# Two segments' scores in one pair of PSUM banks, block means in steps, and a newly computed order

## Chip, core and metric

The kernel runs on one core of one Trainium2 chip. The metric is device time in microseconds (us); three runs of the kernel before gave 614.13, 614.66 and 614.96, median 614.66.

## What is computed

The reference is attention followed by two feed-forward stages, in fp32. q, k and v have 2 batches, 8 heads, 768 positions and 64 elements a head.

```python
block, window = (32, 16)
k_sum = k.reshape(B, H, nb, block, D).max(axis=3)
v_sum = v.reshape(B, H, nb, block, D).mean(axis=3)
scores_l = scale * np.matmul(q, k.transpose(0, 1, 3, 2))
mask_l = np.abs(pos[:, None] - pos[None, :]) < window
scores_s = scale * np.einsum('bhsd,bhnd->bhsn', q, k_sum) + np.log(block)
...
a = softmax over the masked scores_l and the scores_s together
attn = np.matmul(a, np.concatenate([v, v_sum], axis=2))
x = attn.transpose(0, 2, 1, 3).reshape(1536, 512)
...
x = (silu(x @ w_gate) * (x @ w_val)) @ w_out        # 1536 wide inside
h = x @ w_in                                        # 2048 wide inside
out = np.where(h >= 1, h, np.where(h <= -1, 0, (h + 1) ** 2 / 4)) @ w2_out
```

Each position attends to the 31 positions within its window and to 24 block summaries: the maximum of each block of 32 keys, and the mean of each block of 32 values. So a query tile of 64 positions has 96 columns of local scores and 24 columns of block scores (KN = 120).

## The kernel before

**Tiling.** The 1536 rows are three chunks of 512. A chunk consists of two segments of 256 positions (a segment may belong to either batch), and a segment of four query tiles of 64. Heads go in four pairs p = 0 to 3. Chunk 0 goes through attention first; its two feed-forward stages run while TensorE's gaps take the attention of chunks 1 and 2. Afterwards chunks 1 and 2 go through the feed-forward stages together.

**Attention jobs** of batch b, segment s and pair p (`segment_jobs`): sc, the scores (L604: 16 matmuls into two banks, one bank for each head of the pair); mx, mask and maxima (DVE, L617); ex, the exponentials (ACT, L629); iv, sums and reciprocals; no, the normalisation (L642, DVE or POOL); wt, the transposes of the weights (L650, tile pt); pt, their copy out of the bank (tile pT); av, the product with the values (L559, tile px); xh and xl, its copy (tile x) and the remainder (tile xl). Ahead of the first segment of a batch and pair stand kl, ko, kp, kt, km and kc (`head_jobs`): load of the keys, reordering (tile kord), transposes (L496, tile pk), their copies, the block maxima and their broadcast.

**Block means of the values** (`vmean`, tile pv, L468): matmuls with a matrix of averages add up, in one bank, the means of all four pairs, each pair in its own 32 partitions. vo (`vmean_out`) copies a pair's 24 rows out of the bank (four copies a batch, with a ring of three tiles), and ve (`vmean_put`) writes them beside the values of each window (24x1024).

**Weights.** They come as 64-bit numbers. A pack of two 128-wide units is loaded (raw), turned into fp32 by high (ACT, L833), low (ACT or DVE) and bits (DVE, L842, tile wb), kept in DRAM for the later chunks, and split into a rounded part hi and a remainder lo (L865, POOL or DVE, tile wA). Every product is three matmuls: hi with hi, hi with lo, lo with hi (`mm3`, L926). The first pack holds the gate and value units 0 of the first stage, and its products (tiles pg and pv) are 256 columns wide and run for each half of the chunk.

**Order.** Nothing is left to run-time choice: every engine executes its own queue in order. The queues are written by a planner (`Plan.emit`), which takes, again and again, the ready job with the lowest start plus `urge` times rank; ranks are sums of numbers from the table T (L24 on). Jobs that write PSUM take a bank from a ring and give it back when named readers are done: for chunks 1 and 2 all attention jobs share banks b2 and b3, and the products of the weights' columns use b0 and b1 (row products accumulate in y0 to y3). Where the planner expects TensorE to stand idle ahead of a job that takes a bank, it puts transposes of an identity matrix there (`bank`, L296), as fillers.

```python
if engine == "PE" and chosen and len(takes[0]) > 1:
    self.pad = min(self.PAD_MOST, int(max(0.0, idle - self.SLACK) / self.PAD_US))
```

## Time and profile before

| | |
|---|---|
| median of three runs | 614.66 us |
| the profiled execution: time | 613.92 us |
| its span, first to last instruction | 612.2 us |
| busy: TensorE matmul (PE) | 602.9 us, 98% |
| busy: VectorE (DVE) / ScalarE (ACT) / GpSimd (POOL) | 481.8 / 371.3 / 61.8 us |
| TensorE's granted clock, mean | 0.994 |
| chain that ended last | PE 95%, ACT 2%, DVE 1%, POOL 1% |

The page gives one execution of the program. "Busy" counts an instruction from start to end; matmuls overlap, so the cost of one matmul in a row is the distance between starts. An fp32 matmul stands in the trace as two records, so "sc x16" there is 8 matmuls of the program. The chain of the end is followed back from the last instruction: each step to what released it, or to the instruction before it on its engine. The time that is not in the span, 1.7 us here, belongs to the launch.

### The profile page before, as it was taken

Reading aid. Unit: us, or ns where it says so; the run is one execution under the profiler, and the core shown is the slowest. Engines: PE = TensorE matmul, PEld = TensorE weight load, DVE = VectorE, ACT = ScalarE, POOL = GpSimd, SP = SyncE. Lnnn points to the kernel's source line nnn. Section 1 sums busy time; section 2 is a strip of 40 time slices with the busy share of each in tenths; the row PEclk is TensorE's granted clock in tenths of the full one; section 3 lists DMA queues with packets and bytes.
Section 4 is the critical chain, followed back from the end, with each engine's and each line's share of the span. In section 5 each row is a group of like instructions: output and inputs, shape, how many; then the busy total and the mean of one; then the engine's idle time right before and its main releaser. Section 6 shows DMA issues by size and latency. Waiting matters only on the chain.

```text
span 612.2 us, 9565 instructions
## 1 busy us (share of the span) xinstructions
PE 602.9 (98%) x3583; PEld 496.1 (81%) x3583; DVE 481.8 (79%) x869; ACT 371.3 (61%) x670; POOL 61.8 (10%) x73
## 2 busy tenths in 40 slices
PE   7999999999999999999999999999999999999997
PEld 6888877787778888888888888888888888888886
DVE  6689789788889999898897788867798975846662
ACT  6798887787987794665544453532268575646212
POOL 5131012012000000010010000100010220100000
PEclk9799999999999999999999999999999999999999
DMA  9999998779874997123210213233211111013311
GB/s 226 293 324 237 345 323 285 269 268 293 307 278 147 312 349 255 69 77 130 70 69 1 69 70 103 104 103 104 70 34 70 37 67 34 35 34 112 130 35 69
DMA packets 77150, 94.99 MB, mean 155 GB/s; under 512 B 34224, under 2 KB 60080, under 8 KB 77104
## 3 DMA queue, kind: packets, MB, share of 16 engines
q1 hardware_dynamic: 77104, 94.39, 48.7%
q8 instruction: 28, 0.46, 0.3%
q14 instruction: 18, 0.15, 0.1%
HBM read 73.40 MB, written 20.97 MB: 154 GB/s over the span
## 4 chain that ended last, share of the span: by engine, by line
PE 95%; ACT 2%; DVE 1%; POOL 1%; issue 0%; ACTq 0%; POOLq 0%; DVEq 0%
PE acc_y L926 38%; PE qi L926 12%; PE qg L926 9%; PE qv L926 9%; PE pi L926 7%; PE pv L926 6%; PE pg L926 6%; PE pt L650 2%; PE px L559 2%; PE sc L604 1%; PE pk L496 1%; ACT big L629 1%; PE pq L540 1%; ACT big L385 1%; PE pk L296 1%; POOL wA L865 0%
## 5 line engine op out<-in xcount | busy, mean ns | idle before, releaser
L926 PE MATMUL acc_y<-dd,h 128*128 128x512 f32 (+1 forms) x387 | 88.7, 387 | 0.0
L926 PEld LDWEIGHTS acc_y<-dd,h 128*128 128x128 f32 x387 | 72.4, 188 | 14.9
L926 PE MATMUL acc_y<-h,dd 128*128 128x512 f32 x288 | 66.4, 389 | 0.0
L926 PEld LDWEIGHTS acc_y<-h,dd 128*128 128x128 f32 x288 | 54.1, 188 | 11.2
L385 ACT ACTIVATE dd<-wf 128x1024 fp32r<-128x1024 f32 x28 | 29.5, 1056 | 54.8 <-PE acc_y L926 54.8
L926 PE MATMUL acc_y<-wA,h 128*128 128x512 f32 x192 | 45.9, 390 | 0.0
L926 PE MATMUL qi<-xj,wjs 128*128 128x512 f32 x192 | 45.4, 390 | 0.0
L926 PE MATMUL pi<-y,wA 128*128 128x512 f32 x128 | 42.6, 393 | 0.0
L842 DVE SCALAR_TENSOR_TENSOR wb<-dd 128x1024 int32<-128x1024 int32 x34 | 41.4, 1220 | 1.4 <-ACT dd L833 0.7
L865 DVE TENSOR_TENSOR wA<-wb,wA 128x1024 fp32r<-128x1024 f32 x32 | 39.5, 1234 | 3.6 <-ACT wA L385 2.9
L926 PEld LDWEIGHTS qi<-xj,wjs 128*128 128x128 f32 x192 | 36.0, 188 | 7.8 <-DVE xj L865 0.4
L926 PEld LDWEIGHTS acc_y<-wA,h 128*128 128x128 f32 x192 | 36.0, 188 | 7.5
L833 ACT ACTIVATE dd<-raw 128x1024 f32<-128x1024 f32 x34 | 38.7, 1140 | 1.1 <-DMA raw<-in_moe_w_out_dram 0.9
L926 PE MATMUL acc_y<-h,wA 128*128 128x512 f32 x144 | 37.0, 401 | 0.0
L926 PE MATMUL qg<-xj,wjs 128*128 128x512 f32 x144 | 36.3, 390 | 0.0
L926 PE MATMUL qv<-xj,wjs 128*128 128x512 f32 x144 | 36.2, 389 | 0.0
L926 PE MATMUL pg<-x,wA 128*128 128x512 f32 (+1 forms) x112 | 35.9, 375 | 0.3 <-POOL wA L865 0.3
L926 PE MATMUL pv<-x,wA 128*128 128x512 f32 (+1 forms) x112 | 35.7, 375 | 0.0
L926 PE MATMUL qi<-xj,wjo 128*128 128x512 f32 x144 | 35.1, 389 | 0.0
L865 POOL TENSOR_TENSOR dd<-wf,dd 128x1024 fp32r<-128x1024 f32 x5 | 12.8, 2553 | 198.9 <-ACT dd L385 133.5
L865 DVE TENSOR_TENSOR h<-r,h 128x512 fp32r<-128x512 f32 x42 | 30.1, 717 | 2.8 <-ACT h L385 1.8
L926 PEld LDWEIGHTS qg<-xj,wjs 128*128 128x128 f32 x144 | 27.0, 188 | 5.8 <-DVE xj L865 0.2
(165 smaller groups left out, 1263.2 us busy)
## 6 DMA issues: line engine op xcount, KB each, us to landing
raw<-in_moe_w_out_dram SPq DMA_DIRECT2D x14, 1024.0 KB, 7.3
raw<-in_moe_w_in_dram SPq DMA_DIRECT2D x16, 512.0 KB, 5.6
wf<-kept_z SPq DMA_DIRECT2D x16, 512.0 KB, 3.2
raw<-in_moe_w_gate_dram SPq DMA_DIRECT2D x12, 512.0 KB, 6.2
raw<-in_moe_w_val_dram SPq DMA_DIRECT2D x12, 512.0 KB, 7.1
kept_g<-wb SPq DMA_DIRECT2D x12, 512.0 KB, 5.8
wj<-kept_g SPq DMA_DIRECT2D x12, 512.0 KB, 4.7
wf<-kept_o SPq DMA_DIRECT2D x12, 512.0 KB, 3.3
```

The costliest lines, as they stand in the source:

```text
L296: nc.tensor.transpose(t[:, 0:P], ident, ident)
L385: nc.scalar.activation(out, in_, AF.Copy, scale=scale)
L496: nc.tensor.transpose(cols[:, r], kraw[b, p][one, r].rearrange("p h d -> p (h d)"), ident[one, one])
L540: nc.tensor.transpose(pq[:, r * P:(r + 1) * P], raw[:, r].rearrange("p h d -> p (h d)"), ident)
L559: nc.tensor.matmul(px[h * D:(h + 1) * D, col:col + QT], vwin[0:KN, w, 2 * p + h], pT[0:KN, 2 * h + w // 2, w % 2 * QT:(w % 2 + 1) * QT], s ...
L604: nc.tensor.matmul(scs[h][j * QT:(j + 1) * QT, w // 2], qT[head, (w + j) * QT:(w + j + 1) * QT], kwin[p][head, s * WPS + w + j], start=Tru ...
L629: nc.scalar.activation(sm[:, w], sm[:, w], AF.Exp, bias=mx[:, 0, w:w + 1], scale=-1.0, **more)
L650: nc.tensor.transpose(pt[0:KN, w * P:(w + 1) * P], v_["sm"][:, w], ident)
L833: nc.scalar.activation(x[:, 0], raws[k][:, :, :, 1].bitcast(F32), AF.Prelu, scale=2.0 ** -112, alpha=2.0 ** 32)
L842: nc.vector.scalar_tensor_tensor(b, x[:, 0], 3, x[:, 1], op0=ALU.logical_shift_left, op1=ALU.bitwise_or)
L865: e.tensor_tensor(out, a, b, op=ALU.subtract)
L926: nc.tensor.matmul(dst, lhs(a), rhs(b), start=first and i == 0, stop=last and i == 2, **more)
```

## The change

1. **Scores.** Segment (1, 2, p) puts its scores behind those of (1, 1, p) in the same two banks, and (0, 2, p) for p = 1 to 3 behind those of (1, 0, p-1) (`beside`). The second job takes no bank, is ranked directly behind the first, and the banks come free when the maxima of both are done. (0, 2, 0) and (1, 0, 3) have no partner, and the segments of chunk 0 are left as they were.
2. **Means.** For batch 0 the matmuls of the means are three jobs, one for each loaded segment of values and one for the rest, in one bank that is held meanwhile. The matrices of averages are 32 columns wide instead of 24, so that all 128 partitions of the bank are written, and vo is one copy of 128x128 for a batch; its ring of tiles is gone.
3. **Order.** All numbers of T are new but those of `rings`, `handoff`, `order`, `pack` and `wide`, so every queue is in a new order.

The core of the diff (line numbers of L468 and below move by 1 to 8, those of the weights' code by 30):

```diff
--- before.py
+++ after.py
@@ -23,76 +23,76 @@
 T = {'rings': {'sm': 4, 'raw': 3, 'dd': 2, 'wf': 3, 'wA': 4, 'h': 3},
...
- 'urge': 0.00048,
- 'weight': (0.57, 8.439, 0.171, 0.404),
+ 'urge': 0.00044,
+ 'weight': (0.581, 190.813, 0.102, 0.425),
...
@@ -284,7 +284,7 @@
     BANKS, ACCS = ("b0", "b1", "b2", "b3"), ("y0", "y1", "y2", "y3")
     plan = Plan({
         **{r: 1 for r in (*BANKS, *ACCS, *SLOTS)}, "kraw": 2, "kord": 1,
-        "qT": 2, "vm": 3, **T["rings"],
+        "qT": 2, **T["rings"],
     })
     job = plan.job
 
@@ -335,10 +335,10 @@
         return out
 
     carved = carve(
-        "big0", (NPAIR, (NTILE, KN)), (1, (3, KN)), (1, (2 * NB,)), (4, (WPS, 2)),
+        "big0", (NPAIR, (NTILE, KN)), (1, (3, KN)), (4, (WPS, 2)),
         (2, (WPS, KN + 1)))
-    kwin, masks, tavg = carved[:NPAIR], carved[NPAIR], carved[NPAIR + 1]
-    dens, smx = carved[NPAIR + 2:NPAIR + 6], carved[NPAIR + 6:]
+    kwin, masks = carved[:NPAIR], carved[NPAIR]
+    dens, smx = carved[NPAIR + 1:NPAIR + 5], carved[NPAIR + 5:]
     smx += [const.tile([P, WPS, KN + 1], F32, name=f"sm{i}") for i in range(2, T["rings"]["sm"])]
     nc.vector.memset(masks[:, :, KW:], LN_BLOCK / scale)
     nc.vector.memset(masks[:, :, 0:KW], 0.0)
@@ -353,8 +353,8 @@
                     base=WINDOW + sgn * off, pattern=[[-sgn, KW]], channel_multiplier=sgn,
                 )
     carved = carve(
-        "big1", (1, (2 * WPS, H, D)), (2, (CH,)), (2, (2, S // P, D)), (3, (2 * D,)), (1, (2, 2 * NB)))
-    vall, qTs, kraws, vms, wavg = carved[0], carved[1:3], carved[3:5], carved[5:8], carved[8]
+        "big1", (1, (2 * WPS, H, D)), (2, (CH,)), (2, (2, S // P, D)), (2, (2 * D,)), (1, (2, NB + 32)), (1, (NB + 32,)))
+    vall, qTs, kraws, vms, wavg, tavg = carved[0], carved[1:3], carved[3:5], carved[5:7], *carved[7:]
     vwins = [vall[:, i * WPS:(i + 1) * WPS] for i in range(2)]
     nc.vector.memset(wavg, 0.0)
     nc.vector.memset(tavg, 0.0)
@@ -362,7 +362,7 @@
         averages(wavg[:, i, NB:NB + QT // BLOCK], BLOCK, QT // BLOCK, off)
     averages(tavg[:, NB:NB + 2 * P // BLOCK], BLOCK // 2, 2 * P // BLOCK, 0)
 
-    n_raw, n_vm = [0], [0]
+    n_raw = [0]
     n_steps, n_jobs = [0], [0]
     half_b = const.tile([P, 1], F32, name="half_b")
     nc.vector.memset(half_b, 0.5)
@@ -448,39 +448,40 @@
                 in_=v[b, x * n:(x + 1) * n, at:at + 2 * P].rearrange("h (p t) d -> p h (t d)", t=2),
             )
 
-    def vmean(b, tag):
-
-        pv = pend["pv", b] = bank(tag, "pv")
-        parts = []
+    def vmean(b, step, *tags):
+
+        if tags:
+            pend["pv", b] = bank(tags[0], "pv")
+        pv, parts = pend["pv", b], []
         for i in range(HELD[b] * WPS):
             at = NB - i * QT // BLOCK
             vwin = vwins[(b * NSEG + i // WPS) % 2]
             parts.append((
-                wavg[0:KW, min(i, 1), at:at + NB],
+                wavg[0:KW, min(i, 1), at:at + 32],
                 lambda p, vwin=vwin, i=i: vwin[0:KW, i % WPS, 2 * p:2 * p + 2]))
         for at in range(HELD[b] * SEG, S, 2 * P):
             n = NB - at // BLOCK
             for t in range(2):
-                parts.append((tavg[:, n:n + NB], lambda p, at=at, t=t: vraw[b, at, 2 * p * HALVES // H][
+                parts.append((tavg[:, n:n + 32], lambda p, at=at, t=t: vraw[b, at, 2 * p * HALVES // H][
                     :, 2 * p % (H // HALVES):2 * p % (H // HALVES) + 2, t]))
         for i, (w, x) in enumerate(parts):
+            if not b and min(i // WPS, HELD[b]) != step:
+                continue
             for p in range(NPAIR):
                 nc.tensor.matmul(
-                    pv[32 * p:32 * p + NB, 0:2 * D].rearrange("p (h d) -> p h d", h=2), w, x(p),
+                    pv[32 * p:32 * p + 32, 0:2 * D].rearrange("p (h d) -> p h d", h=2), w, x(p),
                     start=i == 0, stop=i == len(parts) - 1, skip_group_check=True,
                 )
 
-    def vmean_out(b, p, engine):
-        t = pend["vm", b, p] = vms[n_vm[0] % 3]
-        n_vm[0] += 1
-        copy(engine, t[KW:KN], pend["pv", b][32 * p:32 * p + NB, 0:2 * D])
+    def vmean_out(b, engine):
+        copy(engine, vms[b], pend["pv", b][:, 0:2 * D])
 
     def vmean_put(b, p, i, engine):
         n = WPS if b else 2 * WPS
         out = vall[KW:KN, i * WPS:i * WPS + n, 2 * p:2 * p + 2]
         copy(
             engine, out.rearrange("p w h d -> p w (h d)"),
-            pend["vm", b, p][KW:KN].unsqueeze(1).to_broadcast([NB, n, 2 * D]),
+            vms[b][32 * p:32 * p + NB].unsqueeze(1).to_broadcast([NB, n, 2 * D]),
         )
 
 
@@ -577,16 +578,16 @@
             x[1][:, cols], pend.pop(("px", c, p, i))[:, cols], x[0][:, cols].bitcast(F32),
             op=ALU.subtract)
 
-    flat = {}
+    flat, shared = {}, {}
 
     def values_out(c, p, engine, ring):
         x = flat[1, c, p] = slot(ring, f"xf{p}")
         copy(engine, x, pend.pop(("px", c, p)))
 
-    def stages(b, s, p, wide):
+    def stages(b, s, p, wide, first=None):
 
         c, col = divmod(b * S + s * SEG, CH)
-        v_ = {}
+        v_ = shared[b, s, p] = {}
 
         def scores(*tags):
             qT = pend["qT", c, p][:, col:col + SEG]
@@ -595,8 +596,12 @@
             n_scores[0] += 1
             v_["mx"] = ap_.tile([P, 2, WPS], F32, tag="mx", name="mx", bufs=4)
             v_["den"] = dens[n_scores[0] % len(dens)]
+            if first is None:
+                v_["banks"] = [bank(tag, "sc") for tag in tags[:2]]
+            at = 0 if first is None else 2 * KN
             scs = v_["sc"] = [
-                bank(tag, "sc")[:, 0:2 * KN].rearrange("p (w c) -> p w c", c=KN) for tag in tags[:2]]
+                x[:, at:at + 2 * KN].rearrange("p (w c) -> p w c", c=KN)
+                for x in (v_ if first is None else shared[first])["banks"]]
             for w in range(0, WPS, 2):
                 for j in range(2):
                     for h in range(2):
@@ -692,16 +697,22 @@
             m = len(rests(b))
             job(("vl", b), {"DMA": (0.45 * m, 1.0 * m, m)}, t + T["vl"][b],
                 lambda _, *rings: load_vrest(b, rings), (), (XF,) * m, after=after)
-            job(("vm", b), {"PE": (2.25, 1.8)[b]}, t + T["vm"][b], lambda e, tag: vmean(b, tag),
-                [("vl", b)] + [("wl", b, s) for s in range(HELD[b])], (banks,),
+            steps = HELD[b] if not b else 0
+            for i in range(steps):
+                job(("vm", b, i), {"PE": 0.9}, t + T["vm"][b],
+                    lambda e, *tags, i=i: vmean(b, i, *tags),
+                    [("wl", b, i)] + ([("vm", b, i - 1)] if i else []), () if i else (banks,))
+            job(("vm", b), {"PE": (0.45, 1.8)[b]}, t + T["vm"][b],
+                lambda e, *tags: vmean(b, steps, *tags),
+                [("vl", b)] + [("wl", b, s) for s in range(HELD[b])]
+                + ([("vm", b, steps - 1)] if steps else []), () if steps else (banks,),
                 [(("vl", b), i) for i in range(m)])
-        job(("vo", *n), {"DVE": 0.25, "ACT": 0.27}, t + T["vo"][b], lambda e, _: vmean_out(b, p, e),
-            [("vm", b)], (("vm",),), [(("vm", b), 0)])
+            job(("vo", b), {"DVE": 0.25, "ACT": 0.27}, t + T["vo"][b], lambda e: vmean_out(b, e),
+                [("vm", b)], (), [(("vm", b, 0) if steps else ("vm", b), 0)])
         for i in range(2 if b else 1):
             job(("ve", *n, i), {"POOL": 0.9, "ACT": 0.62, "DVE+": 0.43} if b else {"POOL": 1.8, "ACT": 1.1, "DVE+": 0.75}, t + T["ve"][b],
                 lambda e, i=i: vmean_put(b, p, i, e),
-                [("vo", *n)] + [("av", *x) for x in last_values.get((p, i), ())], (),
-                [(("vo", *n), 0)])
+                [("vo", b)] + [("av", *x) for x in last_values.get((p, i), ())])
 
     def step_jobs(c, p, t, banks, after):
 
@@ -753,16 +764,34 @@
         job(("f", 1, *n), {"ACT": 0.61, "DVE": 0.7}, t + T["st_xh"][c > 0],
             lambda e, ring: values_out(c, p, e, ring), [("av", *n)], (XF,), [(("av", *n), 0)])
 
+    def beside(b, s, p):
+
+
+        if (b, s) == (1, 2):
+            return (1, 1, p)
+        return (1, 0, p - 1) if (b, s) == (0, 2) and p else None
+
+    def following(b, s, p):
+        return next((x for x in ((1, 2, p), (0, 2, p + 1)) if p + 1 < NPAIR + (x[0] == 1)
+                     and beside(*x) == (b, s, p)), None)
+
     def segment_jobs(b, s, p, t, banks, done):
-        n = (b, s, p)
+        n, one = (b, s, p), beside(b, s, p)
+        held = one or n
         c = (b * S + s * SEG) // CH
         more = {"sc": [("kt", b, p, 0), ("kt", b, p, 1), ("kc", b, p), ("qt", c, p)]}
-        takes = {"sc": (banks, banks, ("sm",)), "wt": (banks, ("s18", "s19") if c else ("s18", "s19", *SLOTS[20:24]))}
-        gives = {"sc": done, "mx": [(("sc", *n), 0), (("sc", *n), 1)], "wt": [(("sc", *n), 2)],
+        if one:
+            more["sc"] = [("sc", *one)]
+        two = following(b, s, p)
+        if two:
+            more["sc"] += [("qt", 1, two[2])] if two[0] == 0 else []
+        takes = {"sc": () if one else (banks, banks, ("sm",), ("sm",)) if two else (banks, banks, ("sm",)), "wt": (banks, ("s18", "s19") if c else ("s18", "s19", *SLOTS[20:24]))}
+        gives = {"sc": done, "mx": [(("sc", *held), 0), (("sc", *held), 1)],
+                 "wt": [(("sc", *held), 3 if one else 2)],
                  "pt": [(("wt", *n), 0)]}
         wide = n_jobs[0] < T["wide"]
         n_jobs[0] += 1
-        fns = stages(b, s, p, wide)
+        fns = stages(b, s, p, wide, one)
         for name, engines, dt, needs in STAGES:
             fn = fns[name]
             if name == "su" and not wide:
@@ -771,7 +800,8 @@
                 engines = {"ACT": 0.95}
             if wide and name == "iv":
                 engines, needs = {"DVE": 0.18}, ("su",)
-            job((name, *n), engines, t + T[dt][c > 0],
+            rank = plan.jobs["sc", *one][1] + 0.1 if one and name == "sc" else t + T[dt][c > 0]
+            job((name, *n), engines, rank,
                 (lambda e, *tags, fn=fn: fn(*tags)) if "PE" in engines else lambda e, *_, fn=fn: fn(e),
                 [(x, *n) for x in needs] + more.get(name, []),
                 takes.get(name, ()), gives.get(name, ()),
```

**PE, chunk 0's first stage with attention of chunk 1 between (sc scores, pq transposes of queries, pk of keys, pt of weights, acc_y row products, pv column products).** Before:

```order
L540 MATMUL pq<-ident,qraw 128x128 x4
L926 MATMUL acc_y_1117<-h,wA 128x512 x3
L926 MATMUL acc_y_1118<-h,wA 128x512 x3
L604 MATMUL sc<-big_78,big_119 64x120 x8
L926 MATMUL acc_y_1130<-h,wA 128x512 x3
L926 MATMUL acc_y_1131<-h,wA 128x512 x3
L650 MATMUL pt<-ident,sm_79 120x128 x4
```

and with the change:

```order
L609 MATMUL sc<-big_78,big_119 64x120 x16
L956 MATMUL pv<-x_678,wA 128x512
L956 MATMUL pv<-xl_691,wA 128x512
L956 MATMUL pv<-x_678,wA 128x512
L956 MATMUL pv<-x_764,wA 128x512
L956 MATMUL pv<-xl_766,wA 128x512
L956 MATMUL pv<-x_764,wA 128x512
L956 MATMUL acc_y_1095<-h,wA 128x512 x3
L956 MATMUL acc_y_1096<-h,wA 128x512 x3
L497 MATMUL pk<-ident,kord 128x80 x6
L497 MATMUL pk<-ident,kord 128x64 x6
```

Eight matmuls of one segment stood alone and others stood alone some products later; now sixteen of two segments stand in one piece. In the whole program, behind the first product, scores were 16 pieces of 8 and are 7 pieces of 16 and 2 of 8; all short work was 50 excursions from the products and is 42, of which those with scores, keys, values or means directly behind products were 30 and are 21.

**ACT, the stretch in which the first weights arrive (dd from raw is the first step of a weight, L629/L634 exponentials, 24x8x128 the means beside the windows).** Before:

```order
L833 ACTIVATE dd<-raw 128x1024
L385 ACTIVATE big_119<-pq 128x512
L385 ACTIVATE big_119<-pv 24x128 x2
L385 ACTIVATE pT<-pt 120x512 x2
L385 ACTIVATE big_119<-pv 24x128
L385 ACTIVATE big_119<-big_119 24x8x128
L629 ACTIVATE sm_79,big_78<-sm_79,mx 128x120 x4
L385 ACTIVATE x_643<-px 128x256 x2
L385 ACTIVATE x_669<-px 128x256
```

and with the change:

```order
L863 ACTIVATE dd<-raw 128x1024
L385 ACTIVATE pT<-pt 120x512 x3
L385 ACTIVATE big_119<-pv 128x128
L385 ACTIVATE big_78<-pk 128x4x96
L385 ACTIVATE big_78<-pk 128x96
L385 ACTIVATE big_119<-big_119 24x8x128 x2
L385 ACTIVATE x_634<-px 128x256
L634 ACTIVATE sm_79,big_78<-sm_79,mx 128x120 x4
L385 ACTIVATE x_673<-px 128x256
L385 ACTIVATE x_678<-px 128x256
L385 ACTIVATE x_634<-px 128x256
```

The first weight's step stood behind the exponentials of pair 2 and ahead of two copies of weights; now it stands ahead of three of them, of a copy of keys' transposes that the scores of pair 3 need, and of two writes of means. The means' copies out of their bank (24x128, four) are one (128x128).

**POOL, from the means to the first weight's remainder (wA).** Before:

```order
L387 TENSOR_SCALAR big_119<-big_119 24x8x128
L865 TENSOR_TENSOR wA<-wb,wA 128x1024
L387 TENSOR_SCALAR kord<-big_119 128x2x6x64
L642 TENSOR_TENSOR sm_79<-sm_79,mx 128x4x120
```

and with the change:

```order
L387 TENSOR_SCALAR big_119<-big_119 24x8x128
L387 TENSOR_SCALAR kord<-big_119 128x2x6x64
L895 TENSOR_TENSOR wA<-wb,wA 128x1024
L647 TENSOR_TENSOR sm_79<-sm_79,mx 128x4x120
L895 TENSOR_TENSOR wA<-wb,wA 128x1024
```

The reordering of the fifth block of keys (kord) stood behind the remainder of the first weight and stands ahead of it; its load is the 29th DMA of SP's queue before, behind the third pair of weight loads, and the 27th now, directly behind the second. The first weight's gate and value loads are the 21st and 22nd in both orders, and the 20 ahead are the same ones, in another order.

## Rows read from the trace of the kernel before

**Rows 1.** The page: its first line, and the chain that ended last, by engine.

```profile
span 612.2 us, 9565 instructions
...
PE 95%; ACT 2%; DVE 1%; POOL 1%; issue 0%; ACTq 0%; POOLq 0%; DVEq 0%
```

**Rows 2.** The chain in order of time: start us, us, what.

```profile
24.66 3.15 ACT big L629 x16
...
387.74 57.12 PE acc_y L926 x252
```

**Rows 3.** Waits of PE, 36 us to the end: total us, times, longest.

```profile
PE pg L926 <- POOL wA L865: 0.3, 1, 0.3
```

**Rows 4.** Timeline of PE, 98 to 113 us: start us, us, what.

```profile
102.49 0.64 PE L604 MATMUL sc<-big,big 64*64 64x120 f32 x16
103.06 0.50 PE L926 MATMUL pv<-x,wA 128*128 128x512 f32 x1
...
105.91 0.60 PE L540 MATMUL pq<-ident,qraw 128*128 128x128 f32 x4
106.27 1.64 PE L926 MATMUL acc_y<-h,wA 128*128 128x512 f32 x6
107.84 0.64 PE L604 MATMUL sc<-big,big 64*64 64x120 f32 x16
```

**Rows 5.** Timeline of PE, 29 to 37 us.

```profile
29.85 1.05 PE L604 MATMUL sc<-big,big 64*64 64x120 f32 x32
30.83 0.77 PE L296 MATMUL px<-ident 128*128 128x128 f32 x5
31.80 2.55 PE L559 MATMUL px<-pT,big 120*64 120x64 f32 x80 [0.20 <-POOL big L387]
...
35.61 0.39 PE L926 MATMUL pg<-x,wA 128*128 128x256 f32 x1
```

**Rows 6.** DMA issues on SP, 18 to 25 us.

```profile
18.24 0.55 SPq L823 DMA_DIRECT2D raw<-in_moe_w_val_dram  x1
...
21.72 2.16 SPq L823 DMA_DIRECT2D raw<-in_moe_w_val_dram  x1
```

**Rows 7.** Line L823 in the window of the issue at 18.24: time to landing.

```profile
DMA to landing us min/median/max: 6.9/6.9/6.9
```

**Rows 8.** The same of the issue at 21.72.

```profile
DMA to landing us min/median/max: 8.0/8.0/8.0
```

**Rows 9.** Timeline of ACT, 24 to 35 us.

```profile
24.02 0.63 ACT L385 ACTIVATE big<-pk 128x384 f32<-128x384 f32 x2
...
27.70 1.18 ACT L833 ACTIVATE dd<-raw 128x1024 f32<-128x1024 f32 x1
...
29.97 1.09 ACT L385 ACTIVATE pT<-pt 120x512 f32<-120x512 f32 x2
31.08 0.27 ACT L385 ACTIVATE big<-pv 24x128 f32<-24x128 f32 x1
31.37 1.05 ACT L385 ACTIVATE big<-big 24x1024 f32<-24x1024 f32 x1
...
34.10 0.94 ACT L385 ACTIVATE x<-px 128x256 fp32r<-128x256 f32 x3
```

**Rows 10.** Timeline of POOL, 34 to 39 us.

```profile
34.05 2.36 POOL L865 TENSOR_TENSOR wA<-wb,wA 128x1024 fp32r<-128x1024 f32 x1 [2.30 <-DVE wA L389]
36.38 0.83 POOL L387 TENSOR_SCALAR kord<-big 128x768 f32<-128x768 f32 x1
37.31 0.99 POOL L642 TENSOR_TENSOR sm<-sm,mx 128x480 f32<-128x480 f32 x1
```

**Rows 11.** Timeline of DVE from 102.9 us: the first of four maxima of a segment.

```profile
103.18 0.28 DVE L617 CUSTOM_DVE_ANT_0 sm<-sc,big 128x120 f32<-128x120 f32 x1 [0.28 <-PE sc L604]
```

**Rows 12.** One of the page's costliest groups: out<-in xcount, busy us, mean ns, idle before.

```profile
L842 DVE SCALAR_TENSOR_TENSOR wb<-dd 128x1024 int32<-128x1024 int32 x34 | 41.4, 1220 | 1.4 <-ACT dd L833 0.7
```

**Rows 13.** Stretch by engine: us, PE busy (count) PEld DVE ACT POOL, PEclk, DMA share, GB/s.

```profile
190.00:260.00 70.00, 70.00 (x336) 57.80 (x336) 64.13 (x86) 48.38 (x64) 0.00 (x0) 1.00 0.68 235
```

More of the change, by code (lines that the diff above doesn't have):

```diff
@@ L86 @@
- 'vm': (-202.741, 183.603),
- 'vs': 412.825,
- 'vo': (-311.865, -1392.846),
- 've': (513.047, 366.626),
- 'ql': (-17.52, 25.88),
- 'wl': (370.144, -88.376),
+ 'd': (5014.082, 26396.924),
+ 'load': (1972.439, 350.381),
+ 'high': (640.33, 330.323),
+ 'bits': (2.83, 129.655),
+ 'keep': (-29797.06, 308.737),
+ 'read': -19117.383,
+ 'hi': (-3195.416, 54.793),
+ 'lo': (2828.882, -922.762),
+ 'head_rank': (1894.837, -5961.185, -8397.057, -198.666),
+ 'half_rank': -1159.508,
+ 'start': 222.03,
+ 'unit': 1.182,
@@ new lines @@
+ 'e0': 83.063,
+ 'a1': (56.723, 13.502),
+ 'a2': (126.63, 18.023),
+ 'x': (1009.377, 332.516),
+ 'j': (979.98, 1683.044),
+ 'g': (0.372, 35.005),
+ 'q': (0.018, 0.072),
+ 'jr': (257.354, 203.651),
+ 'jw': (128.956, 264.892),
+ 'rw': -26.99,
+ 'js': (-18228.294, 1154.238),
+ 'gh': (-389.202, 396.001),
+ 'gl': -560.484,
+ 't': 412.978,
+ 'th': 566.243,
+ 'tl': -294.773,
+ 'qp': (-5.932, 15.462, 10.128, 76.167, 21.613, 19.688, -18.961),
+ 'qf': -154.998,
+ 'qj': -431.952,
+ 'qa': 795.032,
+ 'rs': 1147.804,
@@ new lines @@
+ 'rh': 983.639,
+ 'x2': -20.742,
+ 'r2': (-1237.373, 15572.866),
+ 'first': (-735.298, 570.546),
+ 'st_q': (699.624, 93.123),
+ 'st_qt': (1387.34, -511.652),
+ 'st_sc': (-232.904, -354.64),
+ 'st_mx': (-1598.656, -1398.264),
+ 'st_ex': (-495.363, -449.709),
+ 'st_iv': (-2255.476, -432.616),
+ 'st_no': (243.372, 1494.498),
+ 'st_wt': (31.059, -376.75),
+ 'st_pt': (-1255.703, -10.876),
+ 'st_av': (-599.571, -540.842),
+ 'st_xh': (-216.795, -1505.88),
+ 'st_xl': (-1307.309, -25822.432),
+ 'kl': (-22342.516, -469.333),
```

72 lines of the change are left out of this document (14 added, 58 removed).

## The prediction

> **What bounds the kernel now.** Read first the page's chain by engine: 95% of the 612.2 us span is TensorE [rows 1]. Then ask TensorE's waits after 36 us: the list has one entry, 0.3 us [rows 3]. So from the first product, at 35.6 us [rows 5], to the end TensorE never waits again, and the time is a sum: the head up to the first product, then TensorE's own work, then a tail behind the last matmul whose instructions are the same in both orders. An engine beside it matters only if it comes later than its cover. What TensorE's work costs is read from starts. Undisturbed, 252 matmuls of 512 columns take 57.12 us, 0.2267 us each [rows 2]; half of it, and by starts about 0.12, is one of 256 columns. Where short attention work stands between products, the same view shows a price for the way in and out: 12 products from 103.06 to 105.91 are 2.85 us, 0.13 above 12 x 0.2267; six from 106.27 to 107.84 are 1.57, 0.21 above 1.36 [rows 4]. The second stretch is followed by scores, the first by plain transposes. I read 0.13 us for each return to full products, and 0.08 more where scores, keys, values or means, which run in partial arrays (64*64 in the row), come next.
>
> **The change part by part.**
>
> *TensorE behind the first product (term A).* The matmuls are the same: counted by tile and width, every kind of product and attention matmul has its old number. What changes is how often they alternate. Counted in the two orders, excursions into short work go from 50 to 42: 8 x 0.13 = 1.04 us less. Entries into partial-array work go from 30 to 21: 9 x 0.08 = 0.72 less. Scores: a piece of one segment costs 0.57 (102.49 to 103.06 [rows 4]), a piece of two 0.98 (29.85 to 30.83 [rows 5]), so 16 x 0.57 = 9.12 becomes 7 x 0.98 + 2 x 0.57 = 8.00, 1.12 less. Against it stand two fillers and transposes that are now alone, 0.26 more. **A = -2.6 us**, all on the path, since TensorE has no gaps there to absorb it. The 32-wide averages cost TensorE nothing that I can bound above 0.1: the moving side is still 128 columns.
>
> *The head (term B).* Everything ahead of the first product is the same work in another order, and ACT's queue decides. I walk it with durations of before. The first weight needs its gate and value loads. They stand at the same places of SP's queue behind the same 20 transfers, so the second of them lands where it does now, 18.24 + 6.9 = 25.1 us [rows 6, 7]. ACT's queue in the new order puts the weight's first step, 1.2, behind that landing (before, it stood at 27.7 and did not wait), and behind it three copies of weights 1.6, the means' copy 0.3, the keys' copy 0.6, two writes of means 2.1, and the first x 0.3 [rows 9]: 31.2 us. Then four exponentials 1.55 (half of 3.15 for eight, with their reads [rows 2]), five x at 0.31, the next weight 1.2, four exponentials 1.55, one copy of weights 0.6: 37.7 us.
>
> TensorE meanwhile: scores of pair 3 after the keys' copy at 28.8, to 29.4; the values of three pairs after the first write of means, 96 records at 2.55/80 = 3.1 us [rows 5], to about 32.6; scores 0.57; first product at 33.2, 2.4 earlier than now. Then three waits that before doesn't show. (1) The third product needs the remainder, which is on POOL behind the fifth block of keys. That load stands right behind the second value load, which lands at 21.72 + 8.0 = 29.7 [rows 6, 8]; I add 1.1 for the block, 30.8. Reordering 0.83 and remainder 2.36 [rows 10] give 34.0. The seven products left end at 34.9. (2) The transposes need POOL's next step, 0.99, at 35.0, and end at 35.4; nine products of the second half end at 36.6. (3) The values of pair 3 need the copy of weights, 37.7 as walked, and end at 38.2. Nine products and the transposes of queries end at 39.8. That much work costs 5.1 us at the prices above (27 x 0.12, 1.5 of short work, 0.3 of returns), so this head is worth a first product at 34.7 without waits, against 35.6 + 0.3 now: **B = -1.2 us**. Ends: without the three waits -2.7 (first product 33.2 against 35.9); with ACT two microseconds later than walked +0.8. I take the walk's own value, since the value load's landing, on which it hangs, is measured.
>
> *Behind the head (term C).* DVE gets about 10 us more by count (five roundings, four remainders, three reorderings, five squares more, four normalisations fewer), ACT about 14 less, POOL four remainders fewer and four normalisations more. DVE is the fullest neighbour, 64.1 of 70 us from 190 to 260 [rows 13], but that still leaves 6 of 70, and most of the added work is spread. The means' copies (eight of 0.27 on ACT [rows 9] become two) cost and save nothing outside the head, as TensorE covers them. The three-step means hold their bank longer, in the head alone, where eight banks are shared. I allow **C = +0.4 us** for a wait that I can't place; nothing if before's lack of waits holds, and 2 us if the crowded stretch behind the head slips.
>
> Sum: -2.6 - 1.2 + 0.4 = -3.4 us. Against the profiled execution's own time, 613.92 us, that is 610.5; the median of the runs is 0.74 above that execution, so the forecast is 614.66 - 3.4 = **611.3 us**.
>
> **The rivals.**
>
> *Banks held too long (slower).* The attention of chunks 1 and 2 has only two banks, and a pair's scores occupy both until eight maxima are done instead of four. In the new order the next job that needs one of them stands at the nearest 12 products behind: 0.98 + 0.21 + 2.72 = 3.9 us after the scores begin. DVE began 0.7 us after the scores did (103.18 against 102.49 [rows 4, 11]); eight maxima at 0.28 or less end by 2.9 us. That leaves 1.0 us. If DVE came late by two weight steps of 1.22 us, as bits is [rows 12], TensorE would wait 1.4 us at each of seven pairs, +9.8, and the time would be 614.66 - 3.4 + 9.8 = 621. It decides from a lateness of 1.5 us: 7 x 0.5 eats the gain. For it: DVE's density. Against it: the row shows DVE idle and waiting for the scores, and in the new DVE order the maxima follow at once. The Trainium skill, Perfetto Trace Analysis, section Optimizing Tensor Performance, says that independent groups of matmuls should rotate through different banks, so that one is emptied while the next is computed; this change does the opposite, and by that rule this rival would be the outcome. No wait of before shows a bank as the limit.
>
> *The head gives the gain back (no change).* If the value load lands later, or ACT's queue blocks TensorE longer than walked, each microsecond counts in full: 2.2 to 4.6 us more bring the time to between 613.4 and 615.9, say 614.7. For it: ACT is packed without gaps, and three links hang on it. Against: all durations are measured.
>
> *No new waits in the head.* If the fifth block of keys lands early and ACT keeps ahead, B is -2.7 and C 0: 614.66 - 5.3 = 609.4.
>
> **How the numbers follow.** What a measurement can tell from no change is 0.2%, 1.2 us. Chances: forecast 0.72 (609.5 to 613.4), held banks 0.10, head gives it back 0.13, no new waits 0.05. So faster 0.77, same 0.13, slower 0.10. The range runs from A and B at their low ends with half a microsecond for the price of a switch, 608.8, to B and C at their high ends, 614.66 - 2.6 + 0.8 + 2.0 = 614.9, which I cut to 614.6, since not all of it comes together.
>
> **What would show it.** Right: a first product 1.5 to 3 us earlier; TensorE's waits after it below 3 us and all before 45 us; scores pieces of two at 0.98 us; the last matmul 3 to 4 us earlier. Term A is wrong if the stretch from 50 us to the end of chunk 2's attention does not cost TensorE 2 us less for the same matmuls. B is wrong if the value load does not land near 25 us, or the first x copy is not near 31. The forecast as a whole is wrong if TensorE's waits name maxima (L622) or if waits return behind 60 us.

## The result and the profile after

The changed kernel takes 618.15 us (median of 6 runs, 617.56 to 618.97) against 614.68 us for the kernel before beside it (614.13 to 615.21): a ratio of 1.0057, 95% interval 1.0044 to 1.0070. It is slower by about 3.5 us; the forecast was 3.4 us faster.

The page's first line, and its chain by engine, which answer to [rows 1]:

```profile
span 616.5 us, 9550 instructions
...
PE 93%; ACT 2%; SPq 2%; DVE 2%; DMA 1%; issue 0%; POOL 0%; ACTq 0%; POOLq 0%; DVEq 0%
```

The span grew by 4.3 us. TensorE's share of the chain fell to 93%, but that isn't the loss: it is 93% too in the first experiment below, which is faster, as the chain of the head now goes through loads (SPq, DMA). What TensorE waits for is in the list of TensorE's waits from 32.8 us to the end (us in total, times, longest), where before had one entry of 0.3 us [rows 3]:

```profile
PE sc L609 <- DVE mx L622: 3.8, 6, 0.7
PE pt L655 <- DVE sm L647: 0.7, 1, 0.7
PE pq L541 <- DMA qraw<-in_q_dram: 0.6, 1, 0.6
PE pg L956 <- POOL wA L895: 0.4, 1, 0.4
```

The last three are the head. The first is new and stands six times between 55 and 188 us: scores wait for maxima. Here is one of the six, TensorE's timeline and then VectorE's (start us, us, what, and in brackets the idle time before and its releaser):

```profile
55.52 0.28 PE L956 MATMUL pg<-x,wA 128*128 128x256 f32 x1
55.73 0.64 PE L609 MATMUL sc<-big,big 64*64 64x120 f32 x16
56.98 1.04 PE L609 MATMUL sc<-big,big 64*64 64x120 f32 x16 [0.60 <-DVE mx L622]
57.95 0.39 PE L956 MATMUL pv<-x,wA 128*128 128x256 f32 x1
```

```profile
56.43 0.28 DVE L622 CUSTOM_DVE_ANT_0 big<-sc,big 128x120 f32<-128x120 f32 x1 [1.59 <-PE sc L609]
...
57.04 0.28 DVE L622 CUSTOM_DVE_ANT_0 big<-sc,big 128x120 f32<-128x120 f32 x1
...
58.17 0.28 DVE L622 CUSTOM_DVE_ANT_0 sm<-sc,big 128x120 f32<-128x120 f32 x1 [0.84 <-PE sc L609]
```

(The x16 are 8 matmuls, each with two records. A segment's scores are 8 matmuls, not the 16 that the list of attention jobs gives.) The first segment's scores begin at 55.73. Its maxima begin 0.70 us later, and the second segment's scores begin at 56.98, when the two maxima of the first bank are done, and run 0.97 us instead of 0.41, since the second bank comes free only behind the other two. The pair takes 2.21 us, from 55.73 to 57.95, where 0.98 was forecast. The seven pairs begin at 55.73, 81.92, 103.11, 127.22, 146.93, 161.18 and 186.23 and take 2.21, 2.21, 0.98, 2.32, 2.21, 2.32 and 2.21 us, 14.46 together. In the third VectorE was busy with a weight until 104.3 us, and there alone the order wrote the second scores down ahead of the first maxima.

The order itself says so. These are TensorE's instructions at 55 us with their waits, as the program has them:

```
L609 MATMUL sc<-big_78,big_119 64x120 [waits Activation_49] x2
L609 MATMUL sc<-big_78,big_119 64x120 x6
L609 MATMUL sc<-big_78,big_119 64x120 [waits DVE_49] x2
L609 MATMUL sc<-big_78,big_119 64x120 x6
```

The loop that makes the order writes jobs down in the order of start time plus `URGE` times rank. A pair's second scores start right behind the first (rank 0.1 later), and the first maxima start some 0.3 us after that; but their rank is 1044 lower (`st_mx` -1398 against `st_sc` -355 in the table), which with `URGE` 0.00044 counts as 0.46 us, so they are written down first. They read the two banks that the second scores write. The columns are others, but the bank, and the tile in it, is the same, and the scores that stand behind in the program carry a wait until those reads are done. The kernel's text does not ask for that wait; it is put in when the program is built.

Where the time went is one sum over TensorE's starts (us). A "return" is what a stretch of products takes above 0.2267 us for each of 512 columns and 0.12 for each of 256, so it holds waits among products too. The last column is the first experiment below.

| | before | changed | without the six waits |
|---|---|---|---|
| first product | 35.61 | 32.92 | 33.01 |
| products themselves | 528.37 | 528.37 | 528.37 |
| returns | 9.81 | 8.83 | 9.13 |
| scores | 9.14 | 15.60 | 8.01 |
| transposes of queries | 2.98 | 3.82 | 3.66 |
| all other short work | 22.49 | 23.19 | 23.13 |
| end of the last matmul | 608.39 | 612.72 | 605.29 |

The head came out near the forecast. ACT's timeline, which answers to [rows 9], and three pieces of TensorE's, which answer to [rows 5]:

```profile
24.76 1.14 ACT L863 ACTIVATE dd<-raw 128x1024 f32<-128x1024 f32 x1 [1.48 <-DMA raw<-in_moe_w_val_dram]
...
27.24 0.29 ACT L385 ACTIVATE big<-pv 128x128 f32<-128x128 f32 x1
...
30.24 0.38 ACT L385 ACTIVATE x<-px 128x256 fp32r<-128x256 f32 x1
```

```profile
32.92 0.38 PE L956 MATMUL pg<-x,wA 128*128 128x256 f32 x1
...
33.79 0.50 PE L956 MATMUL pg<-x,wA 128*128 128x256 f32 x2 [0.38 <-POOL wA L895]
...
36.69 0.69 PE L560 MATMUL px<-pT,big 120*64 120x64 f32 x16
```

### The profile page after: what moved, and what is told of

Read it like the earlier page. It is cut to its first block, busy times and chain, and to the rows that moved or that the text cites. A ratio compares the mean times of both kernels' runs of the same rounds, so it can differ in the third digit from the quotient of the medians.

```text
span 616.5 us, 9550 instructions
## 1 busy us (share of the span) xinstructions
PE 602.1 (98%) x3582; PEld 494.8 (80%) x3582; DVE 492.0 (80%) x881; ACT 354.6 (58%) x648; POOL 60.3 (10%) x77
## 4 chain that ended last, share of the span: by engine, by line
PE 93%; ACT 2%; SPq 2%; DVE 2%; DMA 1%; issue 0%; POOL 0%; ACTq 0%; POOLq 0%; DVEq 0%
PE acc_y L956 37%; PE qi L956 12%; PE qv L956 9%; PE qg L956 9%; PE pi L956 7%; PE pv L956 5%; PE pg L956 5%; PE sc L609 2%; PE px L560 2%; SPq L427 1%; PE pt L655 1%; DMA raw<-in_moe_w_val_dram 1%; PE pk L497 1%; ACT big L385 1%; PE pq L541 1%; PE pk L296 1%
## 5 line engine op out<-in xcount | busy, mean ns | idle before, releaser
L385 ACT ACTIVATE dd<-wf 128x1024 fp32r<-128x1024 f32 x26 | 27.5, 1057 | 53.6 <-PE acc_y L956 53.1
L895 DVE TENSOR_TENSOR wA<-wb,wA 128x1024 fp32r<-128x1024 f32 x32 | 41.1, 1284 | 2.8 <-ACT wA L385 1.9
L956 PE MATMUL pv<-x,wA 128*128 128x512 f32 (+1 forms) x112 | 34.3, 369 | 0.0
L895 DVE TENSOR_TENSOR dd<-wf,dd 128x1024 fp32r<-128x1024 f32 x27 | 33.0, 1222 | 0.5 <-ACT dd L385 0.4
L956 PEld LDWEIGHTS qv<-xj,wjs 128*128 128x128 f32 x144 | 27.0, 188 | 5.6
```

The costliest lines, as they stand in the source:

```text
L385: nc.scalar.activation(out, in_, AF.Copy, scale=scale)
L895: e.tensor_tensor(out, a, b, op=ALU.subtract)
L956: nc.tensor.matmul(dst, lhs(a), rhs(b), start=first and i == 0, stop=last and i == 2, **more)
```

## The experiments

Each was compared with the kernel before on its own chip. That kernel took 613.61 us beside the second scores ahead, two of the six, the seventh pair and no sharing; 613.49 beside the change once more, means in one piece, one normalisation earlier and the old numbers; 614.21 beside the mended kernel once more, queries earlier, the need in the plan and the new numbers.

**The second scores written ahead (theory: the six waits are the loss).** Only the place in the program changes; the order on each engine is that of the changed kernel.

```diff
-            fn(engine, *chosen)
-            self.pad = 0
+            calls.append([name, fn, engine, chosen, self.pad])
+            self.pad = 0
+        place = {c[0]: i for i, c in enumerate(calls)}
+        place.update({n: place[one] + 0.5 for n, one in self.behind.items()})
+        for name, fn, engine, chosen, self.pad in sorted(calls, key=lambda c: place[c[0]]):
+            fn(engine, *chosen)
+            self.pad = 0
...
+            if one and name == "sc":
+                plan.behind[name, *n] = ("sc", *one)
```

> Every engine's instructions in the order of the changed kernel; the one edit is that the scores of a pair's second segment are written down ahead of the maxima of its first, so the second eight matmuls have nothing of VectorE's to wait for. Theory (the loss is six waits inside the pairs): the six pieces of 2.21 and 2.32 us become 0.98, the list of TensorE's waits loses the entry on the maxima, the seven pieces together go from 14.46 to 6.9 us, and the time falls by about 7.6, to 610.5 us (609.8 to 611.3). Rival 1 (banks held too long): now eight maxima stand behind sixteen matmuls, the wait moves to the next user of the two banks, and the time stays above 613. Rival 2 (the lost time lies elsewhere, VectorE or the transfers being the limit anyway): the gaps reopen behind the pairs and the time stays above 616.

Measured: 610.76 us (610.50 to 611.59), ratio 0.9958 (0.9942 to 0.9974), faster than the kernel before. The first pair, TensorE and VectorE:

```profile
55.81 1.05 PE L616 MATMUL sc<-big,big 64*64 64x120 f32 x32
56.79 0.39 PE L965 MATMUL pv<-x,wA 128*128 128x256 f32 x1
```

```profile
56.91 0.28 DVE L629 CUSTOM_DVE_ANT_0 big<-sc,big 128x120 f32<-128x120 f32 x1 [2.00 <-PE sc L616]
...
58.34 0.28 DVE L629 CUSTOM_DVE_ANT_0 sm<-sc,big 128x120 f32<-128x120 f32 x1
```

All seven pairs take 0.98 us, 6.87 together, and TensorE's waits from 32.9 us are three, all in the head:

```profile
PE pt L662 <- DVE sm L654: 1.0, 1, 1.0
PE pg L965 <- POOL wA L904: 0.4, 1, 0.4
PE pq L548 <- DMA qraw<-in_q_dram: 0.4, 1, 0.4
```

The same work from 45.6 us to the last attention matmul's end, us and TensorE's busy time (count), then PEld, DVE, ACT, POOL, clock, DMA share and GB/s. First the changed kernel, then this one:

```profile
45.59:208.39 162.80, 158.98 (x1243) 127.88 (x1241) 135.37 (x297) 125.90 (x262) 23.68 (x20) 1.00 0.90 285
```

```profile
45.67:200.95 155.28, 155.28 (x1242) 126.76 (x1240) 135.12 (x297) 125.72 (x262) 23.76 (x20) 1.00 0.95 299
```

The theory holds: 7.5 us less for the same instructions. Rival 1 falls with it. The maxima now begin at 56.91 and the last of the eight ends near 58.6, while the next user of those banks, the means of batch 1, stands 24 products behind, at 59.85; no pair's next user waits. Rival 2 falls too: TensorE has no gap left there, at the same clock. (The mended kernel, below, is this one.)

**Two of the six, and a seventh.** The same edit for `b == 0` alone; and the opposite for all pairs, `place["mx", *one[1:]] + 0.5`.

> The same edit for the pairs that join batch 1's first segment with batch 0's third alone, so that four of the six waits stay (the two near 56 and 82 us go). Theory of the six waits: 2 x 1.23 = 2.5 us less than the changed kernel, 615.7 us. If instead what counts is anything that the edit does to the program as a whole, the time comes out at either end, near 610.5 or near 618.2.

> The opposite: in the seventh pair too (near 103 us, the only one of 0.98 us) the second segment's scores are written down behind the first's maxima; the order of every engine stays. There VectorE is busy with a weight until 104.3, so the second eight can begin only near 105.2, against 103.6. Theory: that pair takes about 2.6 us and the time rises by 1.6, to 619.8 us. Rival (VectorE is the limit and TensorE's wait there is made good later): no change, 618.2.

Measured: 616.23 us (615.01 to 617.44), 0.5 above the theory, and 620.22 us (619.80 to 620.78), 0.4 above it; the first lies between the two ends, the second above the change, as the theory has them. The seventh pair, the only one that is added, as TensorE's timeline of the second kernel has it:

```profile
104.07 0.64 PE L616 MATMUL sc<-big,big 64*64 64x120 f32 x16
105.68 1.04 PE L616 MATMUL sc<-big,big 64*64 64x120 f32 x16 [0.97 <-DVE mx L629]
106.65 0.50 PE L965 MATMUL pv<-x,wA 128*128 128x512 f32 x1
```

It takes 2.58 us, 1.60 more. From the first product to the last matmul, where differences of the head between runs don't enter, the program costs in us:

| waits in pairs | seven pairs | first product to last matmul | median |
|---|---|---|---|
| 0 | 6.87 | 572.28 | 610.76 |
| 4 | 12.00 | 577.28 | 616.23 |
| 6 (the change) | 14.46 | 579.81 | 618.15 |
| 7 | 16.06 | 581.32 | 620.22 |

The third column follows the second to within 0.2 us: here a wait that makes a pair 1.2 to 1.6 us longer is paid in full, and nothing behind makes it good.

**The change and the mended kernel once more, on other chips.**

> The changed kernel itself once more, beside the next three, so that differences of one or two microseconds are read on one chip. Theory of the six waits: its last matmul ends 7.4 us behind that of the kernel without them, and its seven pairs take 14.5 us. The median should be 617 to 618.5 us.

> The kernel without the six waits once more, beside the next three on one chip. Theory: 610.0 to 611.5 us, 0.4 to 0.6% less than the kernel before, seven pairs at 0.98 us, and behind the first product 572.3 us to the last matmul's end, as the first time.

Measured: 618.66 us (ratio 1.0084, 1.0068 to 1.0100) and 611.28 us (0.9964, 0.9951 to 0.9976). The pairs take 14.46 and 6.87 us again, first product to last matmul 579.74 and 572.22.

**No sharing.** `beside` returns None, so every segment's scores take the two banks anew.

> The changed kernel with each segment's scores in banks of their own (no pairs); table of numbers and means in steps as in the change, the order is computed anew and has the same head up to the third piece of products. TensorE has 49 excursions in place of 43, 16 score pieces of 8, and 12 more fillers. Theory (the head is worth what it was worth, and only the wait inside the pairs costs): 16 x 0.57 for scores, 6 x 0.21 for returns and 1.5 for fillers more than a pairing without waits, so 610.5 + 1.1 + 1.3 + 1.5 = 614.4 us, well below the changed kernel, with no wait on maxima in TensorE's list. Rival (the new head or the new table costs the time, not the pairs): 617 us or more.

Measured: 619.04 us (618.36 to 619.66), 4.6 above what the theory gave. The number is the rival's; the place is not. The first product comes at 32.51 us, so the head is sound; 580.74 us lie behind it, against 572.28 with sharing and no waits. Of the 8.5 us more, scores are 3.1 (11.09 for 8.01), fillers 2.4 and returns 2.6. Two of its waits are:

```profile
PE sc L296 <- DVE mx L622: 1.0, 1, 1.0
PE pt L296 <- DVE mx L622: 0.8, 1, 0.8
```

L296 is the filler ahead of a job that takes a bank. At these two places, from 174 to 177 us, the new numbers still put two segments close together, and without sharing the second one waits for the banks as such. The expectation had counted fillers and returns, but not that a filler stands where a wait is. The 8.5 us are not the price of sharing alone, since the order is another too: with sharing, no wait and an order computed anew (the need in the plan, below) the same stretch takes 577.25 us, 3.5 less than here. How much of the rest is order stays open.

**Means in one piece.** In the mended kernel the two early steps stand directly ahead of the last one on TensorE; nothing else moves.

```diff
+        place.update({("vm", 0, i): place["vm", 0] - 0.5 + i / 10 for i in range(2)})
```

> The kernel without the six waits, with one part of the change undone: the first batch's means stand in one piece, the two early steps (32 matmuls, 1.0 us each) directly ahead of the last. All other orders stay. If the steps carry the head, the means' copy on ScalarE (27.3 us) and with it the first product (33.0) come 0.5 to 1.0 us later and the time is 611.3 to 611.8 us. Rival (the early matmuls only filled idle time that is also there later): the copy moves by less than 0.3 us and the time stays at 610.8.

Measured: 613.15 us (611.84 to 615.05), ratio 0.9999 (0.9985 to 1.0012). The first product comes at 34.15 us. The means' copy stands at 27.67, but ACT waited 1.25 us for it, as the first weight's step was done 1 us sooner in this run; and among the value matmuls TensorE pauses 1.35 us with no releaser shown. So the steps are worth about 1 us at the first product and 2 in the median, more than the theory gave. The trace shows only the first of these: it is of the fastest of the twelve runs (611.84 us), and behind its first product it costs 572.15 us, as the mended kernel does. How much belongs to the pause, and what the other runs lost, stays open.

**One normalisation earlier.** In the mended kernel's head one VectorE instruction is moved ahead of a weight's two steps.

```diff
+        place["no", 0, 1, 3] = place["iv", 0, 1, 3] + 0.5
```

> The kernel without the six waits, with one instruction moved: the normalisation of the last weights of the head (0.66 us alone, 2.70 us where it ran beside GpSimd's remainder of a weight, 38.74 to 41.44) stands directly behind its inverses, ahead of a weight's two steps, so it runs before GpSimd begins. Theory (it was slow because of what ran beside it, and TensorE's wait of 0.98 us at 41.59 hangs on it): it takes 0.7 us, the wait goes, 0.9 us less, 609.9 us. Rival (the weight's steps, now 0.7 us later, hold up the remainder and the products behind): the wait moves there, 610.8.

Measured: 610.18 us (610.00 to 610.85), ratio 0.9949 (0.9932 to 0.9967). VectorE in the changed kernel, and then here:

```profile
38.65 2.71 DVE L647 TENSOR_TENSOR sm<-sm,mx 128x480 f32<-128x480 f32 x1
41.28 1.21 DVE L872 SCALAR_TENSOR_TENSOR wb<-dd 128x1024 int32<-128x1024 int32 x1
```

```profile
37.13 0.66 DVE L655 TENSOR_TENSOR sm<-sm,mx 128x480 f32<-128x480 f32 x1
...
39.90 3.27 DVE L882 SCALAR_TENSOR_TENSOR wb<-dd 128x1024 int32<-128x1024 int32 x1
```

The wait of 1.0 us is gone and first product to last matmul is 571.26, 1.0 less, as expected. But in this run the first product came 0.5 us later (33.50), and the wait of 0.4 us for the remainder went with that, so to the last matmul's end 0.5 us is gained. The medians differ by 0.6 us on different chips, and the two ratios' intervals overlap: the wait is shown to go, the gain in the time is not shown.

**Queries earlier.** As the last, and one write moved behind four loads on the DMA queue.

```diff
+        place["keep", "g", 0] = place["ql", 1, 0] + 0.5
```

> The kernel with the head's last normalisation ahead, and on the DMA queue the first write of a weight (kept_g) put behind the next four loads of queries, so those are issued some 1 us earlier. Theory: TensorE's waits for queries near 38.7 and 39.5 us (0.6 together) go and the time falls by 0.5 us against the kernel without this, to 609.7 us. Rival: those loads share the engines with the loads ahead of them and land no earlier: no change, 610.2 us.

Measured: 610.64 us (609.72 to 611.11), ratio 0.9946 (0.9932 to 0.9961). The waits for queries are gone, but first product to last matmul is 571.23, as without the edit: one of 0.3 us for a remainder of x stands in their place. No gain is shown.

**The wait removed by a need in the plan.** The order is computed anew with it.

```diff
         if two:
+            more["mx"] = [("sc", *two)]
             more["sc"] += [("qt", 1, two[2])] if two[0] == 0 else []
```

> The waits removed in another way: the table of jobs says that a pair's first maxima need the second segment's scores, and the order of everything is computed anew with that. All seven pairs then have the second scores ahead, the head up to the third piece of products is the same, but the order behind it is another (173 rows of TensorE differ), with 45 excursions in place of 43 and 11 more fillers where it foresees idle time. Theory: pairs at 0.98 us, no wait on maxima inside a pair, and 610.8 + 2 x 0.13 + 11 x 0.11 = 612.3 us (611 to 613.5). Rival (the gain came from that one order, and a new order loses it again): 614 us or more.

Measured: 616.25 us (615.38 to 617.70), the rival's number. The pairs take 6.87 us, and no scores wait for maxima. Behind the head TensorE now waits for weights and an activation:

```profile
PE acc_y L957 <- DVE wA L896: 1.2, 1, 1.2
PE qg L957 <- ACT qu L385: 0.7, 1, 0.7
PE pg L957 <- DVE wA L896: 0.5, 1, 0.5
```

First product to last matmul is 577.25: 5.0 us of gain lost again by another order of the same work. Of them 2.4 are these three waits and 1.4 are fillers.

**Old numbers with the new code, new numbers with the old code.** The table `T` is exchanged, nothing else.

> The change's code with the table of numbers of the kernel before: pairs, steps and one copy are there, the order is computed anew and gives other orders than either kernel. In it all seven second segments stand ahead of the first's maxima, so none has VectorE to wait for. Counted against the kernel before: 10 excursions fewer (1.3 us), scores 1.1 us less, 0.7 for fewer entries into partial arrays, and 24 more fillers (2.7 us, where the order foresees idle time): about the time of before, 613 us (611.5 to 615), and no piece of two segments over 1.1 us. Rival (sharing banks costs by itself, as the rule that groups should rotate through banks says): waits at the next users of the banks and 616 us or more.

> The other half of the change: the code of the kernel before with the new table of numbers, the order computed anew from it. No pairs, means in one piece and four copies. 48 excursions behind the first product, 16 score pieces of 8, some 14 fillers. The old table with the new code gave 630.6 us, first product at 40.7. If numbers and code go only together, this too is slower than either kernel, 617 to 630 us, with the head's first product later than 36 us or fillers and waits on maxima behind it. Rival (the new numbers are better in themselves): 613 us or less.

Measured: 630.57 us (629.75 to 633.14) and 617.98 us (617.02 to 620.23). The first missed its expectation by 17 us. Its seven pairs take 0.98 us each, so sharing costs nothing inside them; its first product comes at 40.68 us, and among its waits from 36 us are:

```profile
PE pi L956 <- DVE yl L1038: 3.9, 1, 3.9
PE sc L609 <- ACT big L385: 2.6, 1, 2.6
PE pg L296 <- DVE u L1006: 1.8, 1, 1.8
PE pg L956 <- DVE mx L622: 1.2, 1, 1.2
PE pq L296 <- DVE mx L622: 0.7, 1, 0.7
```

Only the last two have to do with banks that scores hold, one in the head and one at 130 us, behind a segment that has no partner. From the first product to the last matmul it takes 583.54 us, 10.8 more than before, in waits, fillers and more returns. TensorE's granted clock fell as well: to 0.50, the lower of its two levels, from 41.24 and again from 194.84 us, for 3.4 us each, behind waits of 2.6 and 1.2 us and of 3.9 us; products of 512 columns then start 0.42 us apart instead of 0.23.

The second kernel came inside its range of times: first product at 35.67 us, and 575.78 us behind it against 572.77 before, the difference being fillers (6.0 us for 2.9). That it would be slower than either kernel did not come: it takes no longer than the change. Each half alone is slower than the kernel before, in the one order that it gives.

## Why the prediction was wrong

**The step that failed** is in term A: "a piece of two 0.98 (29.85 to 30.83 [rows 5]), so 16 x 0.57 = 9.12 becomes 7 x 0.98 + 2 x 0.57 = 8.00, 1.12 less". The row is two segments in four banks of their own, in the head. It could not show a wait between two segments in the same two. Measured, the scores went from 9.14 to 15.60 us, 7.6 more than forecast, and without the six waits they are 8.01, as forecast. The price could have been bounded from before: the maxima begin 0.7 us behind the scores [rows 4, 11], and the last of the four ends 0.9 us later still. This is the fourth in VectorE's timeline of before, where the first began at 103.18:

```profile
103.79 0.28 DVE L617 CUSTOM_DVE_ANT_0 sm<-sc,big 128x120 f32<-128x120 f32 x1
```

With 0.6 for the second segment's own scores that makes 2.2 us for a pair, which is what was measured.

**The rival that was nearest** had the two banks "held too long", and its mechanism was the right kind at the wrong place. It asked whether the next user, 12 products behind, would wait; the next user was the other half of the same pair, at no distance. There the wait needs no lateness of VectorE at all. The sign that the text named, TensorE's waits naming the maxima at L622, came.

The Trainium skill, PSUM — Partial Sum Buffer, section PSUM bank collisions raise a hardware error, says that two engines may not touch the same bank and partitions at once even at other columns, and that semaphores should guard the bank and not the address. By that rule a write of the second scores that stands behind the first's reads has to wait for them, and all six pairs show that the program waits so; the prediction weighed another rule (rotation of banks) and missed this one. What the chip would do without the wait no run here shows, as none lets the two engines meet in a bank, and none puts two tiles into one bank, so whether the wait goes by bank or by tile stays open too.

**Term A otherwise** held in the main. From the table, before against the kernel without waits: scores -1.13 (forecast -1.12). Returns without the waits among them, 9.51 to 9.13 - 0.45 - 0.98 = 7.70, -1.81 (forecast -1.76). Queries without their wait +0.27, and other short work and fillers +0.64, together 0.91 (forecast 0.26). A is -2.0 against -2.6; what was too small was the term for fillers and lone transposes. With every wait taken out, what lies behind the first product did cost 2 us less. With the waits of the head in it, it cost 0.5 less (572.28 against 572.77), so most of what the mended kernel gains lies ahead of its first product.

**Term B** held in its size, in part by luck. The value load was there at 24.76 (walked 25.1), the first x was done at 30.62 (31.2), the first product began at 32.92 (33.2), the third at 33.79 (34.0), the values of pair 3 at 36.69 (37.7). The walk's own sum is 0.3 short: the first write of means ends at 28.8 + 1.05 = 29.9, so with 3.1 for the values and 0.57 for scores the first product comes at 33.5. Of the three waits that it had after that, 1.5 us in all, only the first is in TensorE's list, with 0.38 us; the other two are not. Two came that the walk did not have, 0.56 us for queries and 0.66 for a normalisation, and they make up the sum: first product -2.69, waits in the head 1.60 against 0.3, together -1.4 us, forecast -1.2.

One thing in the profile of before bears on these 2.69 us, and the prediction did not read it. TensorE's granted clock there was 0.50, the lower of its two levels, from 15.94 to 22.76 us, as two stretches of 10 us show by their means (0.80 and 0.86, the third number from the end):

```profile
10.00:20.00 10.00, 7.73 (x76) 6.60 (x76) 8.16 (x45) 8.02 (x23) 3.18 (x3) 0.80 1.12 226
20.00:30.00 10.00, 9.61 (x160) 8.46 (x163) 6.07 (x27) 8.63 (x30) 0.18 (x1) 0.86 1.09 342
```

TensorE had stood idle for 1.7 us before 15.04 and 0.5 before 16.21. Four transposes' records took 1.1 us there (18.03) and 0.65 at 15.04, and the chain that ended last goes through TensorE from 16.2 to 22.3 us. The changed kernel's trace has no such stretch ahead of its first product. So a part of the 2.69 us may be that one execution's clock; no trace of the kernel before without it was kept. The gain as a whole does not hang on it: the runs of before whose mean clock was 0.999 or more, which leaves no room for such a stretch, have medians of 612.9 and 614.4 us beside the mended kernel's 610.76 and 611.28.

**Term C** had put +0.4 us on "a wait that I can't place". In the mended kernel there is none behind the head, as in before. The sum without the pairs' waits is -3.1 us by the two traces, against -3.4: the forecast describes the kernel without the six waits, which runs 2.9 us faster than before on both chips on which it was measured.

## What to carry to other kernels

When two pieces of work are put into one PSUM bank, ask what stands between them in the program. In this kernel the second write waited for the reads of the first that were written down ahead of it, though the columns were others, and TensorE, which was the bound, paid that in full. Write all matmuls of a shared bank down before the first read; here that alone turned 0.6% slower into 0.4% faster with the same order on each engine. An order that is computed anew to the same end is another matter: it lost the gain again. Read the waits that each instruction carries, not only the order, and take the price of a piece from a row with the same sharing of banks.

## What was not expected of the hardware

A VectorE instruction with both inputs in SBUF that starts beside GpSimd's remainder of a weight ended only behind it. The normalisation of 128x480 took 2.71 us from 38.65, GpSimd's from 38.48:

```profile
38.48 2.37 POOL L895 TENSOR_TENSOR wA<-wb,wA 128x1024 fp32r<-128x1024 f32 x1 [3.79 <-DVE wA L389]
```

Moved ahead, it took 0.66, and another that then stood beside GpSimd's remainder, a weight's step of 1.2 us, took 3.27:

```profile
39.73 2.36 POOL L905 TENSOR_TENSOR wA<-wb,wA 128x1024 fp32r<-128x1024 f32 x1 [5.12 <-DVE wA L397]
```

They ended 0.51 and 1.08 us behind GpSimd's end (41.36 against 40.85, 43.17 against 42.09), a little under their own length: by these numbers they did not share with GpSimd but stood still until it was done. With one input in PSUM (px) there is no such wait. In the kernel before, three remainders of x take their usual 0.4 us each while GpSimd's remainder runs from 34.05 to 36.41 [rows 10]:

```profile
34.52 1.09 DVE L576 TENSOR_TENSOR xl<-px,x 128x256 fp32r<-128x256 f32 x3 [0.62 <-ACT x L385]
```

The Trainium skill, SBUF — State Buffer, section Who interferes with whom, says that a VectorE instruction with two inputs in SBUF and a GpSimd one that reads SBUF shut each other out for a whole instruction; the traces agree.
